# Start-up loads put in another order, and the bf16 copy of W1 made by casts inside DRAM

## The chip, the cores and the metric

The kernel runs on one core of a Trainium2 chip. The metric is the device time of one execution in microseconds (us). The engines are TensorE (PE in the profile; PEld is its weight load), VectorE (DVE), ScalarE (ACT), GpSimd (POOL) and SyncE (SP). GpSimd and SyncE issue the transfers here.

## The reference, cut to what matters

Grouped-query attention over 8 batches (16 query heads, 4 key/value heads, 384 tokens, head size 64), then a residual MLP block on the 1024 features:

```python
attn = softmax(q @ k.T / 8) @ v              # per batch and head; x = heads side by side
a1 = alpha1 * x + beta1
u  = x + lam * (w_tok @ a1)                  # token mixing, 384 x 384
a2 = alpha2 * u + beta2
out = u + lam * (relu(a2 @ W1) @ W2)         # W1: 1024 x 4096, W2: 4096 x 1024
```

All inputs are float32. The kernel computes in bf16, so W1, W2, q, k and v have to be cast, and it casts them on their way in, in the transfer.

## The kernel before: the parts that matter

Two Python generators are woven together. `side(b)` is attention, token mixing and the transposes of a2 for batch b; `main(b)` is the MLP of batch b, in two phases, h (a2 @ W1, 16 chunks of W1 in a ring of four buffers) and ch (h @ W2). Batch 0's `side` runs alone; then `main(b)` is woven with `side(b+1)`. W2 stays in SBUF. W1 does not fit, so batch 0 loads it as float32 with a cast and writes a bf16 copy to DRAM, which the later batches read.

```python
def load_qkv(b):
    ...  # k, q (four groups), v: GpSimd transfers that cast
    nc.gpsimd.tensor_copy(out=vt[b % 2][:, :, :, :D], in_=vr)
...
def load_w1(b, c):
    t = sb.tile([P, NDT, CW * P], bf, tag="w1", name="w1", bufs=4)
    if b == 0:
        nc.gpsimd.dma_start(out=t, in_=w1src[:, :, c * CW * P:(c + 1) * CW * P])
        nc.sync.dma_start(out=w1_scr[c], in_=t)
    else:
        nc.sync.dma_start(out=t, in_=w1_scr[c])
    return t
...
with tc.manual_schedule(engines={mybir.EngineType.PE}):
    for _ in side(0):
        pass
    for b in range(B):
        m = main(b)
        if b + 1 < B:
            qkv[b + 1] = load_qkv(b + 1)
            s = side(b + 1)
        if b == 0:
            ...  # W2 in eight pieces, all of it, before any W1 chunk
```

`manual_schedule` fixes the order of TensorE's instructions only. On every other engine the order is chosen when the program is built, from the dependences: an instruction that depends on nothing may be put far ahead of its place in the text. The hardware then executes each engine's list in order: the traces below show engines standing 5.9 to 35.2 us in front of one instruction with the others behind it.

The softmax here doesn't subtract the row's maximum and nothing guards it: scores larger than these inputs give would overflow.

## Time and profile before

| | us |
|---|---|
| median of the runs | 914.5 |
| batch 0's h starts | 72.5 |
| from there to batch 1's h | 128.3 |
| each later batch, from h to h | 104.1 |
| last batch's h to the end | 88.3 |

These rows add up to the span: 72.5 + 128.3 + 6 x 104.1 + 88.3 = 913.7 (913.5 in the trace). "h starts" is the first matmul of the first product for a batch in TensorE's timeline. The 104.1 is TensorE's own work (busy 103.2 of the 104 us from 200 to 304), so the first two rows are where time can be won or lost.

The list of TensorE's waits in the kernel before (what waited, for what; us in all, times, longest) has this line on W1:

```profile
PE h L276 <- DMA w<-in_moe_w_ch_dram: 21.4, 7, 5.5
```

It is by far the largest of TensorE's waits that is not in the first 13 us.

### The profile page before, as it was taken

The numbers are of one execution on the slowest core, as the hardware profiler recorded it, in microseconds if no ns is written. First come the engines' busy times: TensorE is split into PE (matmuls) and PEld (weight loads), VectorE is DVE, ScalarE is ACT, GpSimd is POOL, SyncE is SP. The second block draws the span as 40 slices with busy tenths as digits, with TensorE's granted clock in tenths as the row PEclk, the third lists the DMA queues.
The fourth block names the chain that finished last, engine by engine and source line by source line (L and its number), as shares of the span: only waits on it lengthen the run. The fifth ranks groups of instructions, "written<-read, shape, count | busy, mean of one in ns | idle before, by whom it ended". The sixth has DMA issues, their size and how long they took to land.

```text
span 913.5 us, 13365 instructions
## 1 busy us (share of the span) xinstructions
PE 846.7 (93%) x5753; PEld 470.2 (51%) x5753; DVE 415.6 (45%) x767; ACT 212.3 (23%) x321; POOL 68.1 (7%) x89
## 2 busy tenths in 40 slices
PE   2647778999999999999999999999999999999997
PEld 1414444456654565456654566445654566445543
DVE  2572332564346444464436543464436534372211
ACT  1602232004420243103420143103430044101100
POOL 6402220000000000001000000001000000000000
PEclk9957899999999999999999999999999999999999
DMA  9999997117511554107521455006620244104300
GB/s 197 196 211 204 232 247 205 44 42 189 171 58 44 119 171 147 44 24 184 171 81 44 97 170 170 24 36 157 177 102 24 71 159 155 44 35 154 135 34 37
DMA packets 72475, 109.69 MB, mean 120 GB/s; under 512 B 28640, under 2 KB 45024, under 8 KB 72416
## 3 DMA queue, kind: packets, MB, share of 16 engines
q1 hardware_dynamic: 26064, 82.32, 25.8%
q0 software_dynamic: 46352, 26.51, 21.4%
q8 instruction: 45, 0.74, 0.3%
q14 instruction: 14, 0.11, 0.0%
HBM read 114.36 MB, written 20.97 MB: 148 GB/s over the span
## 4 chain that ended last, share of the span: by engine, by line
PE 82%; DMA 12%; DVE 4%; issue 1%; POOL 0%; ACT 0%; POOLq 0%; ACTq 0%
PE ch L288 36%; PE h L276 31%; DMA w<-in_moe_w_ch_dram 7%; PE sc L203 6%; PE av L160 3%; DMA v_raw<-in_v_dram 3%; PE tok L244 2%; DVE kz L151 2%; DMA w_scr<-w 1%; DMA k_raw<-in_k_dram 1%; PE tp L191 1%; PE tp L262 1%; DVE o L293 1%; DVE k L141 0%; PE tp L146 0%
## 5 line engine op out<-in xcount | busy, mean ns | idle before, releaser
L276 PE MATMUL h<-a2T,w 128*128 128x384 bf16 x2048 | 376.4, 330 | 21.4 <-DMA w<-in_moe_w_ch_dram 21.4
L288 PE MATMUL ch<-w,hT 128*128 128x512 bf16 x1536 | 352.2, 379 | 0.9
L276 PEld LDWEIGHTS <-w 128*128 128x128 bf16 x2048 | 195.8, 99 | 146.3 <-DMA w<-in_moe_w_ch_dram 23.7
L288 PEld LDWEIGHTS <-hT 128*128 128x128 bf16 x1536 | 147.4, 98 | 168.0 <-issue 2.9
L206 ACT ACTIVATE es<-sc 128x768 bf16<-128x768 f32 x192 | 153.9, 809 | 200.3 <-PE sc L203 200.3
L279 ACT ACTIVATE hT<-h 128x384 bf16<-128x384 f32 x128 | 62.7, 490 | 453.0 <-PE h L276 453.0
L281 DVE TENSOR_SCALAR hT<-h 128x384 bf16<-128x384 f32 x128 | 71.3, 557 | 205.0 <-PE h L276 204.2
L203 PE MATMUL sc<-qT,kz 128*128 128x384 bf16 x384 | 95.4, 332 | 4.0 <-DVE qT L195 2.9
L293 DVE TENSOR_TENSOR o<-ch,lam 128x512 f32<-128x512 f32 x48 | 33.1, 690 | 117.2 <-PE ch L288 116.6
L160 PEld LDWEIGHTS <-es 128*128 128x128 bf16 x1152 | 53.2, 99 | 21.7 <-ACT es L206 1.5
L160 PE MATMUL av<-v,es 128*128 128x65 bf16 x1152 | 57.4, 195 | 1.5 <-ACT es L206 0.8
L167 DVE RECIPROCAL rinv<-av 128x6 f32<-128x6 f32 x64 | 12.3, 192 | 90.5 <-PE av L160 90.1
L203 PEld LDWEIGHTS <-kz 128*128 128x128 bf16 x384 | 36.0, 99 | 30.3 <-issue 4.6
L244 PE MATMUL tok<-a,wtokT 128*128 128x512 bf16 x144 | 42.3, 410 | 6.9 <-DVE a L178 6.9
L246 DVE TENSOR_TENSOR x<-tok,x 128x512 f32<-128x512 f32 x48 | 33.0, 689 | 28.3 <-PE tok L244 28.3
L170 DVE TENSOR_TENSOR x<-av,rinv 128x192 f32<-128x192 f32 x128 | 39.7, 352 | 1.9
L294 DVE TENSOR_TENSOR o<-o,x 128x512 f32<-128x512 f32 x48 | 35.8, 747 | 0.9
L87 POOL DMA_DIRECT2D q_raw<-in_q_dram x32 | 23.8, 747 | 149.8 <-DVE q L185 149.7
L178 DVE TENSOR_TENSOR a<-a1f,h 128x768 bf16<-128x768 f32 x32 | 30.6, 958 | 1.5 <-issue 0.5
L177 DVE TENSOR_TENSOR a1f<-x,g 128x768 f32<-128x768 f32 x32 | 30.6, 958 | 1.1
L250 DVE TENSOR_TENSOR a2f<-x,al 128x1024 f32<-128x1024 f32 x24 | 29.4, 1224 | 0.7
L251 DVE TENSOR_TENSOR a<-a2f,be 128x1024 bf16<-128x1024 f32 x24 | 29.3, 1222 | 0.5
(33 smaller groups left out, 221.4 us busy)
## 6 DMA issues: line engine op xcount, KB each, us to landing
w<-w_scr SPq DMA_DIRECT2D x112, 512.0 KB, 3.2
out_dram<-o SPq DMA_DIRECT2D x48, 256.0 KB, 2.0
w<-in_moe_w_ch_dram POOLq DMA_DIRECT2D x8, 1024.0 KB, 19.7
w<-in_moe_w_ch_dram POOLq DMA_DIRECT2D x16, 512.0 KB, 12.1
w_scr<-w SPq DMA_DIRECT2D x16, 512.0 KB, 5.8
q_raw<-in_q_dram POOLq DMA_DIRECT2D x32, 192.0 KB, 4.9
k_raw<-in_k_dram POOLq DMA_DIRECT2D x8, 192.0 KB, 4.3
v_raw<-in_v_dram POOLq DMA_DIRECT2D x8, 192.0 KB, 5.2
```

The lines of the kernel that those rows point to most:

```text
L160: nc.tensor.matmul(out=av[:, hh, sq, :], lhsT=es[sk][:, hh, sq * P:(sq + 1) * P], rhs=vb[:, hk, sk, :], start=(sk == 0), stop=(sk == NST - 1))
L170: nc.vector.tensor_tensor(out=x[:, :, c0:c0 + D], in0=av[:, hh, :, :D], in1=rinv[:, hh].to_broadcast([P, NST, D]), op=MUL)
L203: nc.tensor.matmul(out=sc[:, hh, :S], lhsT=kz[:, hk, hh, sk * P:(sk + 1) * P], rhs=qT[:, p % 2, :], start=True, stop=True)
L206: nc.scalar.activation(out=e, in_=sc[:, :, :S], func=EXP, scale=scale_qk)
L244: nc.tensor.matmul(out=ps, lhsT=wtokT[:, st, tt * P:(tt + 1) * P], rhs=a1[:, st, cs], start=(st == 0), stop=(st == NST - 1))
L246: nc.vector.tensor_tensor(out=x[:, tt, cs], in0=ps, in1=x[:, tt, cs], op=ADD)
L276: nc.tensor.matmul(out=ps[:, :S], lhsT=w1[:, dt, j * P:(j + 1) * P], rhs=a2T[:, dt, :], start=(dt == 0), stop=(dt == NDT - 1))
L279: nc.scalar.activation(out=hT[:, nt, :], in_=ps[:, :S], func=RELU)
L281: nc.vector.tensor_scalar_max(out=hT[:, nt, :], in0=ps[:, :S], scalar1=0.0)
L288: nc.tensor.matmul(out=ps, lhsT=hT[:, nt, ms * P:(ms + 1) * P], rhs=w2[:, nt, cs], start=(nt == 0), stop=(nt == NNT - 1))
L293: nc.vector.tensor_tensor(out=o, in0=ps, in1=lam_t[:, cs], op=MUL)
L294: nc.vector.tensor_tensor(out=o, in0=o, in1=x[:, ms, cs], op=ADD)
```

## The change

The intent: batch 0's q, k and v come first and nothing beside them; half of W2 is loaded before most of W1, the other half between the W1 chunks; the bf16 copy of W1 no longer holds the ring's buffers, since sixteen DRAM-to-DRAM casts make it, written after everything else of the start. The diff, cut to its core:

```diff
-    w1_scr = tc.dram_tile([NCH, P, NDT, CW * P], bf, name="w1_scr")
+    w1_scr = [tc.dram_tile([P, NDT, CW * P], bf, name=f"w1_scr{c}") for c in range(NCH)]
...
-        nc.gpsimd.tensor_copy(out=vt[b % 2][:, :, :, :D], in_=vr)      # in load_qkv
+        nc.vector.tensor_copy(out=vb[:, :, :, :D], in_=vr)             # in side(b)
...
-        nc.sync.dma_start(out=t, in_=src)                              # lam, alpha, beta
+        nc.gpsimd.dma_start(out=t, in_=src)                            # behind q, k, v
...
             nc.gpsimd.dma_start(out=t, in_=w1src[:, :, c * CW * P:(c + 1) * CW * P])
-            nc.sync.dma_start(out=w1_scr[c], in_=t)
...
+    w1_tiles = {c: load_w1(0, c) for c in range(RING)}                 # RING = 4
+    def late_loads():
+        for i in range(4):
+            load_w2(0, i, 4)
+        yield
+        for c in range(RING, NCH):
+            w1_tiles[c] = load_w1(0, c)
+            if c % 2 == 1:
+                load_w2(1, (c - RING) // 2, 8)
+            yield
+        for i in range((NCH - RING) // 2, 8):
+            load_w2(1, i, 8)
+        for c in range(NCH):
+            nc.gpsimd.dma_start(out=w1_scr[c], in_=w1src[:, :, c * CW * P:(c + 1) * CW * P])
...
-    wtok_in = sb.tile([P, NST, S], bf, tag="a1", name="wtok_in", bufs=1)
+    wtok_in = sb.tile([P, NST, S], bf, tag="o", name="wtok_in", bufs=2)
```

Besides, q's transposes are made one group ahead, a1 and a2 in smaller pieces, w_tok's transposes in the middle of batch 0's attention, and `main(0)` calls `next(late)` after each chunk.

More of the change, by code (lines that the diff above doesn't have):

```diff
@@ L56 @@
     NCH = NNT // CW
+    RING = 4
     scale_qk = 1.0 / float(D) ** 0.5
@@ L62 @@
     psum = ST(tc.psum_pool(name="psum", bufs=2))
-    w1_scr = tc.dram_tile([NCH, P, NDT, CW * P], bf, name="w1_scr")
+    w1_scr = [tc.dram_tile([P, NDT, CW * P], bf, name=f"w1_scr{c}") for c in range(NCH)]
     ident = const.tile([P, P], bf, tag="ident", name="ident")
-    make_identity(nc, ident)
     vt = [const.tile([P, Hkv, NST, D1], bf, tag=f"v{i}", name=f"v{i}") for i in range(2)]
-    for t in vt:
-        nc.vector.memset(t[:, :, :, D:], 1.0)
     w2 = const.tile([P, NNT, DM], bf, tag="w2", name="w2")
@@ L75 @@
     kz = const.tile([P, Hkv, 2, S], bf, tag="kz", name="kz")
-    nc.vector.memset(kz[:D, :, 1, :], 0.0)
-    nc.vector.memset(kz[D:, :, 0, :], 0.0)
     wtokT = const.tile([P, NST, S], bf, tag="wtokT", name="wtokT")
+    qkv = {}
     def load_qkv(b):
@@ L88, in load_qkv, with bcast @@
             qr.append(t)
-        vr = sb.tile([P, Hkv, NST, D], bf, tag="v_raw", name="v_raw", bufs=1)
-        nc.gpsimd.dma_start(out=vr, in_=v[b].rearrange("h (p st) d -> p h st d", st=NST))
-        nc.gpsimd.tensor_copy(out=vt[b % 2][:, :, :, :D], in_=vr)
-        return qr, kr
-    def bcast(ap, name, pool, tag, bufs=1):
-        t = pool.tile([P, DM], f32, tag=tag, name=name, bufs=bufs)
+            if g == 0:
+                vr = sb.tile([P, Hkv, NST, D], bf, tag="v_raw", name="v_raw", bufs=1)
+                nc.gpsimd.dma_start(out=vr, in_=v[b].rearrange("h (p st) d -> p h st d", st=NST))
+        qkv[b] = qr, kr, vr
+    def bcast(ap, name):
+        t = const.tile([P, DM], f32, tag=name, name=name)
         src = bass.AP(tensor=ap.tensor, offset=ap.offset, ap=[[0, P]] + [list(x) for x in ap.ap])
-        nc.sync.dma_start(out=t, in_=src)
+        nc.gpsimd.dma_start(out=t, in_=src)
         return t
-    qkv = {0: load_qkv(0)}
-    lam_t = bcast(moe_lam, "lam", const, "lam")
-    g1 = bcast(moe_alpha1, "g1", const, "g1")
-    h1 = bcast(moe_beta1, "h1", const, "h1")
-    nc.gpsimd.tensor_tensor(out=g1, in0=g1, in1=lam_t, op=MUL)
-    nc.gpsimd.tensor_tensor(out=h1, in0=h1, in1=lam_t, op=MUL)
-    al2 = bcast(moe_alpha2, "al2", const, "al2")
-    be2 = bcast(moe_beta2, "be2", const, "be2")
-    wtok_in = sb.tile([P, NST, S], bf, tag="a1", name="wtok_in", bufs=1)
-    nc.gpsimd.dma_start(out=wtok_in, in_=moe_w_tok.rearrange("(p tt) s -> p tt s", tt=NST))
     w1src = moe_w_ch1.rearrange("(dt di) nf -> di dt nf", di=P)
@@ L116, in load_w1 @@
     def load_w1(b, c):
-        t = sb.tile([P, NDT, CW * P], bf, tag="w1", name="w1", bufs=4)
+        t = sb.tile([P, NDT, CW * P], bf, tag="w1", name="w1", bufs=RING)
         if b == 0:
             nc.gpsimd.dma_start(out=t, in_=w1src[:, :, c * CW * P:(c + 1) * CW * P])
-            nc.sync.dma_start(out=w1_scr[c], in_=t)
         else:
@@ L123, in load_w1, with load_w2 @@
         return t
+    def load_w2(dw, i, n):
+        r, cs = slice(i * NNT // n, (i + 1) * NNT // n), slice(dw * 512, (dw + 1) * 512)
+        nc.gpsimd.dma_start(out=w2[:, r, cs], in_=w2src[:, r, cs])
+    load_qkv(0)
+    make_identity(nc, ident)
+    for t in vt:
+        nc.vector.memset(t[:, :, :, D:], 1.0)
+    nc.vector.memset(kz[:D, :, 1, :], 0.0)
+    nc.vector.memset(kz[D:, :, 0, :], 0.0)
+    g1 = bcast(moe_alpha1, "g1")
+    h1 = bcast(moe_beta1, "h1")
+    lam_t = bcast(moe_lam, "lam")
+    nc.vector.tensor_tensor(out=g1, in0=g1, in1=lam_t, op=MUL)
+    nc.vector.tensor_tensor(out=h1, in0=h1, in1=lam_t, op=MUL)
+    wtok_in = sb.tile([P, NST, S], bf, tag="o", name="wtok_in", bufs=2)
+    nc.gpsimd.dma_start(out=wtok_in, in_=moe_w_tok.rearrange("(p tt) s -> p tt s", tt=NST))
+    w1_tiles = {c: load_w1(0, c) for c in range(RING)}
+    al2 = bcast(moe_alpha2, "al2")
+    be2 = bcast(moe_beta2, "be2")
+    def late_loads():
[11 more added lines that the diff above has]
+            nc.gpsimd.dma_start(out=w1_scr[c], in_=w1src[:, :, c * CW * P:(c + 1) * CW * P])
     xs = {}
@@ L132, in side @@
     def side(b):
-        qr, kr = qkv.pop(b)
+        qr, kr, vr = qkv.pop(b)
         vb = vt[b % 2]
@@ L137, in side, with k_transpose @@
         a1 = sb.tile([P, NST, DM], bf, tag="a1", name="a1", bufs=1)
-        for h0 in range(0, Hkv, 2):
+        def k_transpose(h0):
             k2 = sb.tile([P, 2, NST, 2, D], bf, tag="q2", name="k2", bufs=1)
@@ L151, in side, with q_transpose @@
                 nc.vector.tensor_copy(out=kz[r, h0:h0 + 2, i, :], in_=pv[r])
-            yield
-        qT = None
-        av_todo = None
+        def q_transpose(g):
+            q2 = sb.tile([P, 2, NST, 2, D], bf, tag="q2", name="q2", bufs=1)
+            for i in range(2):
+                nc.vector.tensor_copy(
+                    out=q2[:, i],
+                    in_=qr[g][:, 2 * i:2 * i + 2].rearrange("p h st d -> p st h d"))
+            ps = tp_ps([P, 2 * NST, P])
+            for i in range(2 * NST):
+                hp, st = i // NST, i % NST
+                nc.tensor.matmul(out=ps[:, i, :], lhsT=q2[:, hp, st].rearrange("p h d -> p (h d)"),
+                                 rhs=ident, is_transpose=True, start=(i == 0),
+                                 stop=(i == 2 * NST - 1), skip_group_check=True)
+            qT = sb.tile([P, 2, S], bf, tag="qT", name="qT", bufs=2)
+            nc.vector.tensor_copy(out=qT.rearrange("p a b -> p (a b)"),
+                                  in_=ps.rearrange("p a b -> p (a b)"))
+            return qT
         def av_piece(p, es, hh, av):
@@ L171, in norm @@
                                         in1=rinv[:, hh].to_broadcast([P, NST, D]), op=MUL)
-            if p % 2 == 1:
-                sl = slice((p - 1) * P, (p + 1) * P)
-                t = sb.tile([P, NST, 2 * P], f32, tag="tmp", name="a1f", bufs=1)
-                gb = g1[:, None, sl].to_broadcast([P, NST, 2 * P])
-                hb = h1[:, None, sl].to_broadcast([P, NST, 2 * P])
-                nc.vector.tensor_tensor(out=t, in0=x[:, :, sl], in1=gb, op=MUL)
-                nc.vector.tensor_tensor(out=a1[:, :, sl], in0=t, in1=hb, op=ADD)
-        for p in range(NP):
-            if p % 2 == 0:
-                g = p // 2
-                q2 = sb.tile([P, 2, NST, 2, D], bf, tag="q2", name="q2", bufs=1)
-                for i in range(2):
-                    nc.vector.tensor_copy(
-                        out=q2[:, i],
-                        in_=qr[g][:, 2 * i:2 * i + 2].rearrange("p h st d -> p st h d"))
-                ps = tp_ps([P, 2 * NST, P])
-                for i in range(2 * NST):
-                    hp, st = i // NST, i % NST
-                    nc.tensor.matmul(out=ps[:, i, :], rhs=ident,
-                                     lhsT=q2[:, hp, st].rearrange("p h d -> p (h d)"), is_transpose=True, start=(i == 0),
-                                     stop=(i == 2 * NST - 1), skip_group_check=True)
-                qT = sb.tile([P, 2, S], bf, tag="qT", name="qT", bufs=2)
-                nc.vector.tensor_copy(out=qT.rearrange("p a b -> p (a b)"),
-                                      in_=ps.rearrange("p a b -> p (a b)"))
-                yield
+            sl = slice(p * P, (p + 1) * P)
+            t = sb.tile([P, NST, P], f32, tag="a1f", name="a1f", bufs=1)
+            gb = g1[:, None, sl].to_broadcast([P, NST, P])
+            hb = h1[:, None, sl].to_broadcast([P, NST, P])
+            nc.vector.tensor_tensor(out=t, in0=x[:, :, sl], in1=gb, op=MUL)
+            nc.vector.tensor_tensor(out=a1[:, :, sl], in0=t, in1=hb, op=ADD)
+        k_transpose(0)
+        yield
+        qTs = {0: q_transpose(0)}
+        yield
+        nc.vector.tensor_copy(out=vb[:, :, :, :D], in_=vr)
+        av_todo = None
+        for p in range(NP):
             hk = (2 * p) // G
@@ L203, in side @@
                     nc.tensor.matmul(out=sc[:, hh, :S], lhsT=kz[:, hk, hh, sk * P:(sk + 1) * P],
-                                     rhs=qT[:, p % 2, :], start=True, stop=True)
-                e = sb.tile([P, 2, S], bf, tag="es", name="es", bufs=6)
+                                     rhs=qTs[p // 2][:, p % 2, :], start=True, stop=True)
+                e = sb.tile([P, 2, S], bf, tag="es", name="es", bufs=5)
                 nc.scalar.activation(out=e, in_=sc[:, :, :S], func=EXP, scale=scale_qk)
@@ L217, in side @@
                     yield
+                if sk == 1 and p % 2 == 0 and p + 2 < NP:
+                    qTs[p // 2 + 1] = q_transpose(p // 2 + 1)
+                    yield
+                if sk == 0 and p == 1:
+                    k_transpose(2)
+                    yield
+                if sk == 1 and p == 3 and b == 0:
+                    for st in range(NST):
+                        ps = tp_ps([P, NST, P])
+                        wv = wtok_in.rearrange("p tt (s st) -> p tt st s", st=NST)
+                        for tt in range(NST):
+                            nc.tensor.matmul(out=ps[:, tt, :], lhsT=wv[:, tt, st, :], rhs=ident,
+                                             is_transpose=True, start=(tt == 0),
+                                             stop=(tt == NST - 1), skip_group_check=True)
+                        nc.vector.tensor_copy(out=wtokT[:, st, :],
+                                              in_=ps.rearrange("p a b -> p (a b)"))
             av_todo = (p, es, None)
@@ L224, in side @@
         norm(pp, av)
-        if b == 0:
-            for st in range(NST):
-                ps = tp_ps([P, NST, P])
-                wv = wtok_in.rearrange("p tt (s st) -> p tt st s", st=NST)
-                for tt in range(NST):
-                    nc.tensor.matmul(out=ps[:, tt, :], lhsT=wv[:, tt, st, :], rhs=ident,
-                                     is_transpose=True, start=(tt == 0), stop=(tt == NST - 1),
-                                     skip_group_check=True)
-                nc.vector.tensor_copy(out=wtokT[:, st, :], in_=ps.rearrange("p a b -> p (a b)"))
         yield "tok"
@@ L239, in side @@
         for tt in range(NST):
+            a2 = sb.tile([P, NDT, P], bf, tag="a2", name="a2", bufs=2)
+            a2s.append(a2)
             for dw in range(NDW):
@@ L246, in side @@
                 nc.vector.tensor_tensor(out=x[:, tt, cs], in0=ps, in1=x[:, tt, cs], op=ADD)
-                yield
-            a2f = sb.tile([P, DM], f32, tag="tmp", name="a2f", bufs=1)
-            a2 = sb.tile([P, NDT, P], bf, tag="a2", name="a2", bufs=2)
-            nc.vector.tensor_tensor(out=a2f, in0=x[:, tt, :], in1=al2, op=MUL)
-            nc.vector.tensor_tensor(out=a2.rearrange("p a b -> p (a b)"), in0=a2f, in1=be2, op=ADD)
-            a2s.append(a2)
+                a2f = sb.tile([P, 512], f32, tag="a2f", name="a2f", bufs=2)
+                nc.vector.tensor_tensor(out=a2f, in0=x[:, tt, cs], in1=al2[:, cs], op=MUL)
+                eng = nc.vector
+                eng.tensor_tensor(out=a2[:, dw * 4:(dw + 1) * 4, :].rearrange("p a b -> p (a b)"),
+                                  in0=a2f, in1=be2[:, cs], op=ADD)
+                yield
             if tt > 0:
@@ L269, in main @@
         x = xs.pop(b)
+        more = late if b == 0 else None
         for c in range(NCH):
-            w1 = load_w1(b, c)
+            w1 = w1_tiles.pop(c) if b == 0 else load_w1(b, c)
             for j in range(CW):
@@ L282, in main @@
                 yield
+            if more is not None:
+                next(more, None)
         for dw in range(NDW):
@@ L296, in main, with count @@
                 yield
+    def count(gen):
+        return sum(1 for _ in gen)
+    late = late_loads()
+    n_att = 2 + NP * NST + NP * 2 + NP // 2 - 1 + 1
+    n_main = NNT + 4 * NST * NDW
     with tc.manual_schedule(engines={mybir.EngineType.PE}):
@@ L301 @@
         for b in range(B):
-            m = main(b)
             s = None
             if b + 1 < B:
-                qkv[b + 1] = load_qkv(b + 1)
-                s = side(b + 1)
-            if b == 0:
-                for i in range(NNT // 4):
-                    nc.gpsimd.dma_start(out=w2[:, i * 4:(i + 1) * 4, :],
-                                        in_=w2src[:, i * 4:(i + 1) * 4, :])
-            n_main = NNT + 4 * NST * NDW
-            n_side = 2 + NP // 2 + NP * NST + NP * 2
-            done = 0
-            hold = False
+                load_qkv(b + 1)
+            if b == 0:
+                next(late)
+            m = main(b)
+            if b + 1 < B:
+                s = side(b + 1)
+            done, tok = 0, False
             for i, _ in enumerate(m):
@@ L317 @@
                     continue
-                want = min(n_side, (i + 1) * n_side * 14 // (n_main * 10))
-                while not hold and done < want + (1 if hold else 0):
-                    r = next(s, "end")
+                want = (i + 1) * n_att * 14 // (n_main * 10)
+                while not tok and done < want:
                     done += 1
-                    if r == "tok":
-                        hold = True
-                if done >= n_side and i >= n_main * 3 // 4:
-                    hold = False
+                    tok = next(s) == "tok"
+                if tok and i >= n_main * 3 // 4:
                     if next(s, "end") == "end":
```

## The prediction

> **What bounds the kernel now.** I read the page's busy slices first, then the chain of waits, then the timelines of the first 160 us. The slices:
>
> ```profile
> PE   2647778999999999999999999999999999999997
> PEclk9957899999999999999999999999999999999999
> DMA  9999997117511554107521455006620244104300
> ```
>
> A slice is 22.8 us. From slice 7 on TensorE is 90% busy or more: that part is TensorE's own work. The first six slices (137 us) are not, and there DMA stands at 9. So there are two kernels: a start bound by loading, and a long TensorE-bound run. In the chain of waits the groups of main's first product (line 276) start at 200.93, 305.01, 409.09, ... 825.40 us: one batch is exactly 104.08 us (54.1 for h, 50.0 for ch), with 99.2 us of each 100 busy. Nothing in the change touches that rate, so the question is when batch 1 starts its h, and the end follows 713 us later.
>
> The start, from the chain of waits:
>
> ```profile
> 1.27 11.31 DMA k_raw<-in_k_dram
> ...
> 33.12 21.79 DMA w<-in_moe_w_ch_dram
> 55.45 29.93 DMA v_raw<-in_v_dram
> ...
> 91.73 13.58 DMA w<-in_moe_w_ch_dram
> 105.33 5.87 DMA w_scr<-w
> 111.76 11.40 DMA w<-in_moe_w_ch_dram
> ```
>
> The reader is to see three things: the first k takes 11.31 us (the median k takes 4.3); weights are the wait from 33 us on; and from 91 us load, scratch copy and load alternate: a W1 buffer is free again only when its copy to scratch has been written. TensorE's timeline:
>
> ```profile
> 47.16 1.44 PE L244 MATMUL tok<-a,wtokT 128*128 128x512 bf16 x3 [3.23 <-DVE a L178]
> 52.23 4.00 PE L244 MATMUL tok<-a,wtokT 128*128 128x512 bf16 x9 [3.63 <-DVE a L178]
> ...
> 72.48 2.74 PE L276 MATMUL h<-a2T,w 128*128 128x384 bf16 x8 [5.51 <-DMA w<-in_moe_w_ch_dram]
> ```
>
> The token product waits for a1 on VectorE, because wtok_in holds the one "a1" buffer until it is transposed; then h waits for its first W1 chunk, queued behind all of W2. And GpSimd's timeline:
>
> ```profile
> 55.45 0.75 POOL L90 DMA_DIRECT2D v_raw<-in_v_dram  x1 [4.37 <-DMA w<-in_moe_w_ch_dram]
> 85.50 0.83 POOL L91 COPY v<-v_raw 128x768 bf16<-128x768 bf16 x1 [29.30 <-DMA v_raw<-in_v_dram]
> ```
>
> GpSimd stood 29.3 us in front of a copy whose v lay behind the weights in the queue; meanwhile it issued no W1 load.
>
> So batch 0's h starts at 72.48 and batch 1's at 200.93: 128.45 us where a steady batch takes 104.08, **24.4 us too much**. Those 24.4 and what can be cut from the 72.5 are all there is to win.
>
> **What the Trainium skill says.** "DMA: Bandwidth & Descriptors", section "Issuing engines are not separate DMA queues": transfers from any engine share the same 16 DMA engines. The trace agrees: the first k took 11.31 us while five broadcasts from SyncE (0.52 MB each) ran beside it. The same page, "SWDGE vs HWDGE vs iDMA": a cast can be issued only from GpSimd, so W1, W2, q, k, v and the new DRAM casts all stand in one queue and their order is what matters. The same page's Specifications give 435 GB/s as the fabric ceiling. From 50 to 60 us, with casts alone, the windows show 211 to 213 GB/s; that is counted in bf16 as landed (queue 0 shows 26.51 MB, which is W1, W2, q, k, v and w_tok at 2 bytes), so 422 GB/s of float32 read: at that ceiling. "TensorE: Matmul & The Clock Gate", Part 1: after idle windows of about 3.4 us the clock is halved. The trace agrees: granted 0.50 from 45 to 60 us, and three token products took 1.44 us.
>
> **The change, part by part.**
>
> *1. First exp.* It starts at 20.17. k (issued 1.27, median 4.3) should land near 5.6 once the broadcasts queue behind it; the identity now follows six issues of 0.75 us, so it is ready near 6.3. From k's landing to the first exp it was 20.17 - 12.58 = 7.6; the second k transpose moves later, and one such block is 15.44 - 13.02 = 2.4, which leaves 5.2. First exp about 12 (estimate): 8 us won.
>
> *2. Attention of batch 0.* ScalarE ran its 24 exps in 21.3 us (20.17 to 41.45). VectorE's share now has a1 in line: normalising 8 x (0.20 + 0.62) = 6.6; a1 in 16 halves of about 0.5 = 8; three q blocks of 0.60 + 0.55 = 3.5; k 0.61 + 1.12 = 1.7; wtokT 3 x 0.36 = 1.1; the v copy about 0.5. Sum 21.4, as much as the exps. I take 23: end at 35.
>
> *3. Token stage.* From 52.23 to the last copy's end at 67.70 it was 15.5 us, of which VectorE worked 13.5 (6 x 0.69, 6 x 1.22, 3 x 0.69). Halving the a2 pieces shortens only the dependence: 14.5, plus 1.5 for the last a1. h starts at 35 + 1.5 + 14.5 = **51 instead of 72.5: 21.5 us won**. W1's first four chunks (2.1 MB) come after 1.2 of q/k/v, 0.3 of w_tok and three broadcasts, so by about 26 us; they don't hold h.
>
> *4. Main of batch 0.* What must have landed before the last W1 chunk: q/k/v of two batches 2.4, w_tok 0.3, W1 8.4, half of W2 4.2 and six eighths of the other half 3.1, together 18.4 MB at 0.211 = 87 us; five broadcasts, 2.6 MB uncast at twice that rate, 6 us; from 1.3 that is 94.6. TensorE reaches chunk 15 at 51 + 15 x 3.38 = 101.7 (3.38 is 54.1 / 16). So the queue leads by some 7 us at the end; with a ring of four a load has three chunks, 10.1 us, to land, and one takes about 2 x 2.5 + 2. I allow 3 us of stalls: **24.4 - 3 = 21.4 us won**.
>
> *5. Casts to scratch.* They take the place of 16 copies from SBUF (8.4 MB, median 5.8 us each, in the ring's loop). 16 x 0.524 MB / 0.211 = 40 us after W2 is in, near 105: done near 145. Batch 1's main starts at 51 + 107 = 158. Hidden, with 13 us to spare.
>
> *6. The rest.* v's copy moves to VectorE (8 x about 0.5), a1 comes in smaller pieces, es has 5 buffers for 6: VectorE is 48% busy in a steady batch, so no effect; 104.1 stays.
>
> Sum: 914.5 - 21.5 - 21.4 = 871.6, so **872 us**.
>
> **Rivals.**
>
> *The casts go too early.* GpSimd's order is not the program's: v_raw of batch 2 was issued at 55.45, ahead of most of batch 0's W1, since nothing held it. The DRAM casts depend on nothing either. Were all ahead of the late W1 chunks, 40 us of transfers would be added: chunk 15 near 135, a stall of about 33 us, the whole near 902. Against it: the order before looks paced by transfer time (between two q_raw issues only one W2 piece), and the last W1 loads stand ahead in the program. I give it one chance in seven, and some in part.
>
> *The casts are slow or in the way.* No trace shows a DRAM-to-DRAM cast. At twice the time they end near 185; the W1 chunks themselves would still come in time, but batch 2's q and k stand behind them and TensorE, whose order is fixed, would wait up to 30 us at 158: about 895 to 900.
>
> *VectorE bounds the new start.* If its small pieces or their order cost more, h starts at 58 to 60: 880. For it: my 21.4 leaves no slack.
>
> *All is hidden anyway.* Against it: TensorE's idle time lies exactly in these 137 us, and the steady run can't absorb it.
>
> **Range and chances.** An h start between 46 and 57 gives 867 to 878; stalls of 0 to 15 us widen it to 862 to 890; the first two rivals pull the upper end to 896. Faster by over 2% needs under 896.2: 0.83. Within 2%: 0.14. Slower: 0.03, as nothing is added to the TensorE-bound run.
>
> **What would show it.** First exp near 12 us; first h near 51, not waiting for weights; in batch 0's main under 5 us of h waiting for W1; batch 1's h near 158 and each later one 104 us on; DRAM casts only after the last W1 load, done by 145, and no wait on k or q of batch 2. Wrong if casts stand among the W1 loads in GpSimd's timeline, or if VectorE has no idle time up to 35 us and h starts after 58.

## The result, and the profile after

The changed kernel takes **928.1 us** (median of four runs), against 914.3 for the kernel before in the same rounds. The ratio is 1.0152, with a 95% interval of 1.0135 to 1.0170. Ratios here are the mean time of one kernel's fast runs over the mean of the other's fast runs of the same rounds, so not quite the ratio of the medians quoted. The prediction was 872, with 896 as the upper end.

| us | before | predicted | after |
|---|---|---|---|
| batch 0's h starts | 72.5 | 51 | 61.8 |
| from there to batch 1's h | 128.3 | 107.1 | 151.7 |
| each later batch | 104.1 | 104.1 | 104.1 |
| last h to the end | 88.3 | - | 87.8 |

The start won 10.7 us; batch 0's main lost 23.4; the rest is as it was. First the busy slices of the page (TensorE, its granted clock, the transfers), which answer to the three lines shown of before:

```profile
PE   4675765999999999999999999999999999999997
PEclk9867898999999999999999999999999999999999
DMA  9999999205631175205631175105630144104301
```

The loading start is still there, still with a 9 for the transfers in every slice, and TensorE at 4 to 7 of ten in it. The windows of the changed kernel from 80 to 140 us (columns: window, busy time of PE, PEld, DVE, ACT and POOL, granted clock, DMA share, GB/s as landed) show what the transfers did in it:

```profile
80.00:100.00 20.00, 9.48 (x47) 4.89 (x47) 2.95 (x7) 3.42 (x5) 6.17 (x7) 0.66 1.45 198
100.00:120.00 20.00, 13.70 (x99) 8.16 (x100) 4.68 (x11) 4.18 (x7) 6.93 (x8) 0.91 1.45 198
120.00:140.00 20.00, 13.19 (x97) 7.64 (x95) 5.91 (x14) 4.59 (x8) 6.24 (x8) 0.91 1.45 198
```

The rate does not move, 198 GB/s in each window, so I take the queue to be full: 0.524 MB, one piece, every 2.65 us. What was in the queue is told by GpSimd's timeline (start, length, line, operation, in brackets the idle time before it and what ended it). Line 111 is W2, line 143 is a cast to the scratch copy, line 104 a W1 chunk, line 80 the k of batch 2:

```profile
57.97 0.74 POOL L111 DMA_DIRECT2D w<-in_moe_w_ch_dram  x1 [4.33 <-DMA w<-in_moe_w_ch_dram]
60.54 0.85 POOL L143 DMA_DIRECT2D w_scr<-in_moe_w_ch_dram  x1 [1.83 <-DMA w<-in_moe_w_ch_dram]
63.06 0.84 POOL L143 DMA_DIRECT2D w_scr<-in_moe_w_ch_dram  x1 [1.67 <-DMA w<-in_moe_w_ch_dram]
65.59 0.83 POOL L143 DMA_DIRECT2D w_scr<-in_moe_w_ch_dram  x1 [1.69 <-DMA w<-in_moe_w_ch_dram]
68.39 0.91 POOL L104 DMA_DIRECT2D w<-in_moe_w_ch_dram  x1 [1.97 <-PE tp L183]
70.69 0.84 POOL L143 DMA_DIRECT2D w_scr<-in_moe_w_ch_dram  x1 [1.40 <-DMA w<-in_moe_w_ch_dram]
...
126.36 0.84 POOL L143 DMA_DIRECT2D w_scr<-in_moe_w_ch_dram  x1 [1.79 <-DMA w<-in_moe_w_ch_dram]
...
131.90 0.76 POOL L80 DMA_DIRECT2D k_raw<-in_k_dram  x1
...
137.22 0.89 POOL L104 DMA_DIRECT2D w<-in_moe_w_ch_dram  x1 [2.14 <-DMA w<-in_moe_w_ch_dram]
```

The casts, last in the text of the start, are issued from 60.54 to 126.36 us; the last W1 chunk follows at 137.22. All sixteen casts, and all of W2, stand ahead of it. TensorE's timeline at the first chunks that were not there yet:

```profile
61.76 2.72 PE L308 MATMUL h<-a2T,w 128*128 128x384 bf16 x8 [0.78 <-DVE a2T L295]
88.92 2.74 PE L308 MATMUL h<-a2T,w 128*128 128x384 bf16 x8 [10.90 <-DMA w<-in_moe_w_ch_dram]
102.23 2.74 PE L308 MATMUL h<-a2T,w 128*128 128x384 bf16 x8 [3.84 <-DMA w<-in_moe_w_ch_dram]
```

Chunk 4 was issued at 68.39, as soon as its buffer was free, and h waited for it until 88.92: twenty us behind eight pieces of the queue. The first eight matmuls after such a wait take 2.74 us instead of 1.46, at half the clock (granted 0.50 from 89 to 92 us). And the changed kernel's list of TensorE's waits, against the 21.4 us shown of before:

```profile
PE h L308 <- DMA w<-in_moe_w_ch_dram: 27.5, 9, 10.9
PE h L308 <- DVE hT L313: 9.4, 1, 9.4
```

The second line is another thing. h does not wait for VectorE to be done with work but for VectorE to be free, and VectorE's timeline says what held it (line 218 is v's copy, line 162 k's):

```profile
34.36 0.36 DVE L218 COPY v<-v_raw 128x768 bf16<-128x768 bf16 x1 [5.91 <-DMA v_raw<-in_v_dram]
...
152.38 0.61 DVE L162 COPY k<-k_raw 128x384 bf16<-128x384 bf16 x2 [13.24 <-DMA k_raw<-in_k_dram]
```

At 34.36 this is the copy of batch 1's v, in the middle of batch 0's attention; at 152.38 the copy of batch 2's k, in batch 0's main. Both had been put early on VectorE, and VectorE stood in front of them until the transfers landed. The Trainium skill says in "TensorE: Matmul & The Clock Gate", in its table of specifications, that the queues of ScalarE, VectorE and GpSimd are strictly first in, first out; these 5.91 and 13.24 us of standing still agree.

### The profile page after: what moved, and what is told of

Read it like the earlier page. It is cut to its first block, busy times and chain, and to the rows that moved or that the text cites. A ratio compares the mean times of both kernels' runs of the same rounds, so it can differ in the third digit from the quotient of the medians.

```text
span 925.8 us, 13415 instructions
## 1 busy us (share of the span) xinstructions
PE 848.0 (92%) x5706; PEld 473.1 (51%) x5753; DVE 429.2 (46%) x889; ACT 212.0 (23%) x321; POOL 76.9 (8%) x104
## 4 chain that ended last, share of the span: by engine, by line
PE 80%; DMA 14%; DVE 3%; issue 1%; POOL 1%; POOLq 0%
PE ch L322 34%; PE h L308 32%; DMA w<-in_moe_w_ch_dram 7%; PE sc L226 5%; PE av L195 3%; DMA k_raw<-in_k_dram 2%; DMA w_scr<-in_moe_w_ch_dram 2%; PE tok L275 2%; DMA be<-in_moe_beta_dram 2%; DVE o L327 1%; PE tp L183 1%; PE tp L293 1%; DMA h<-in_moe_beta_dram 1%; DVE kz L172 1%; DVE a2f L279 1%
## 5 line engine op out<-in xcount | busy, mean ns | idle before, releaser
L308 PE MATMUL h<-a2T,w 128*128 128x384 bf16 x2048 | 378.4, 331 | 37.6 <-DMA w<-in_moe_w_ch_dram 27.5
L322 PE MATMUL ch<-w,hT 128*128 128x512 bf16 x1490 | 347.4, 379 | 6.6 <-DVE o L327 3.2
L195 PEld LDWEIGHTS <-es 128*128 128x128 bf16 x1152 | 53.9, 100 | 29.3 <-DVE x L205 7.7
L211 DVE TENSOR_TENSOR a1f<-x,g 128x384 f32<-128x384 f32 x64 | 35.6, 557 | 1.8
L212 DVE TENSOR_TENSOR a<-a1f,h 128x384 bf16<-128x384 f32 x64 | 35.6, 556 | 1.8
L281 DVE TENSOR_TENSOR a<-a2f,be 128x512 bf16<-128x512 f32 x48 | 33.0, 690 | 1.4
L279 DVE TENSOR_TENSOR a2f<-x,al 128x512 f32<-128x512 f32 x48 | 32.9, 688 | 1.0
L328 DVE TENSOR_TENSOR o<-o,x 128x512 f32<-128x512 f32 x48 | 33.0, 687 | 0.7
## 6 DMA issues: line engine op xcount, KB each, us to landing
w<-in_moe_w_ch_dram POOLq DMA_DIRECT2D x24, 512.0 KB, 20.4
```

What stands on the lines that cost most here:

```text
L195: nc.tensor.matmul(out=av[:, hh, sq, :], lhsT=es[sk][:, hh, sq * P:(sq + 1) * P], rhs=vb[:, hk, sk, :], start=(sk == 0), stop=(sk == NST - 1))
L211: nc.vector.tensor_tensor(out=t, in0=x[:, :, sl], in1=gb, op=MUL)
L279: nc.vector.tensor_tensor(out=a2f, in0=x[:, tt, cs], in1=al2[:, cs], op=MUL)
L308: nc.tensor.matmul(out=ps[:, :S], lhsT=w1[:, dt, j * P:(j + 1) * P], rhs=a2T[:, dt, :], start=(dt == 0), stop=(dt == NDT - 1))
L322: nc.tensor.matmul(out=ps, lhsT=hT[:, nt, ms * P:(ms + 1) * P], rhs=w2[:, nt, cs], start=(nt == 0), stop=(nt == NNT - 1))
```

## The experiments

Two theories followed from this. A: sixteen casts of 2.65 us each in front of the late W1 chunks are the loss. A': besides, VectorE is held by copies whose data stand behind the weights. The rivals: the ring of four is too short for loads that take 20 us to land (B), or W2's second half, which also went ahead of chunk 4, is to blame (C). All twelve runs gave correct results. They ran in four groups on different chips (1 to 4, 5 to 8, 9 to 11, and 12); the kernel before, timed beside each group, took 913.0 to 914.2 us, so medians of different groups compare to about 1 us.

| kernel | median us | ratio to before | h of batch 0 | to batch 1's h | later batches |
|---|---|---|---|---|---|
| before | 913.0 to 914.5 | 1 | 72.5 | 128.3 | 104.1 |
| after | 928.1 | 1.0152 | 61.8 | 151.7 | 104.1 |
| 1 casts held back | 897.8 | 0.9827 | 62.1 | 121.4 | 104.1 |
| 2 GpSimd in written order | 944.8 | 1.0347 | 61.4 | 145.1 | 104.1 to 113.3 |
| 3 no scratch copy | 899.4 | 0.9844 | 62.1 | 121.4 | 104.1 |
| 4 scratch copy from SBUF | 913.1 | 0.9992 | 67.0 | 133.0 | 104.1 |
| 5 k and v copies held | 939.0 | 1.0286 | 56.4 | 155.6 | 106.0 |
| 6 casts, and copies held | 899.4 | 0.9851 | 56.1 | 118.5 | 106.0 |
| 7 written order, copies held | 897.9 | 0.9835 | 56.5 | 111.6 | 111.6, then 106.0 |
| 8 before, with casts | 936.9 | 1.0258 | 73.5 | 151.1 | 104.1 |
| 9 all three held | 889.8 | 0.9730 | 55.8 | 116.9 | 106.0, then 104.1 |
| 10 and constants early | 885.7 | 0.9696 | 54.4 | 116.7 | 106.0, then 104.1 |
| 11 half the casts | 915.8 | 1.0021 | 60.8 | 136.6 | 104.1 to 105.8 |
| 12 four W2 pieces ahead | 889.7 | 0.9732 | 51.6 | 121.4 | 106.0, then 104.1 |

**1. The casts held back.** `tc.issue_after` adds an order on the issuing engine and no wait for completion:

```diff
+            with tc.issue_after(last_w1[0]):      # batch 0's last W1 load
                 nc.gpsimd.dma_start(out=w1_scr[c], ...)
```

> The changed kernel with one edge added: the sixteen DRAM-to-DRAM casts may be issued only after batch 0's last W1 load. Theory A (the casts stand among the late W1 loads and each 0.5 MB of them delays the next chunk by about 2.6 us, 40 us in all): h's wait for W1 falls from 27.5 us to under 10, batch 1's h starts near 170 instead of 213.6, total 880 to 890. Rival B (a ring of four with loads that land 20 us after issue is the limit whatever stands in the queue): h still waits over 20 us and the total stays above 905. Rival C (W2's second half, still ahead of chunk 4, is what delays): one wait of some 7 us at chunk 4 stays, the rest goes.

897.8 us: 30.3 us less than the changed kernel, and all of it between batch 0's h and batch 1's (151.7 to 121.4). No wait of h for W1 is left in TensorE's list, so B falls: the ring of four is enough when the queue holds only what is needed (run 7 shows it without the long wait that follows here). C's 7 us did not show either, since something else came first. One wait is left, here in TensorE's timeline and then VectorE's:

```profile
80.81 0.82 PE L186 MATMUL tp<-ident,q 128*128 128x128 bf16 x6 [14.36 <-DVE q L180]
```

```profile
78.98 0.37 DVE L221 COPY v<-v_raw 128x768 bf16<-128x768 bf16 x1 [16.94 <-DMA v_raw<-in_v_dram]
```

VectorE stood 16.94 us in front of batch 2's v, whose transfer had been issued at 60.71 behind W2. That is why the total stayed above the 880 to 890 that I expected.

**2. GpSimd in the order of the text.**

```diff
-    with tc.manual_schedule(engines={mybir.EngineType.PE}):
+    with tc.manual_schedule(engines={mybir.EngineType.PE, mybir.EngineType.Pool}):
```

> The changed kernel with GpSimd's instructions kept in the order in which the program is written: W2's second half goes between the W1 chunks and the casts come last. Theory A: as with the casts held back, 875 to 888; if W2's second half ahead of chunk 4 matters too (rival C), some 7 us less than the run with the casts held back alone. Rival B: above 905. A risk: q of batch 1 holds GpSimd up before W2 is issued.

944.8 us, the slowest of all, where I had expected 875 to 888, though W1's waits are down to 3.6 us in all, with the casts last and W2's second half between the chunks. From its list of waits:

```profile
PE tok L275 <- DVE x L277: 32.7, 1, 32.7
PE h L308 <- DVE hT L313: 19.8, 5, 6.8
PE h L308 <- DMA w<-in_moe_w_ch_dram: 3.6, 3, 1.5
```

Batch 2's k, q and v now came after sixteen casts (k issued at 156.24), but VectorE's list, still ordered by the build, had the copies of that k and v ahead of batch 1's token stage:

```profile
175.29 0.35 DVE L162 COPY k<-k_raw 128x384 bf16<-128x384 bf16 x1 [35.15 <-DMA k_raw<-in_k_dram]
```

VectorE stood still for 35.15 us. The order of one engine had been fixed and the other engine's had not followed. The six later batches together lost 27 us more (651.8 against 624.6 in run 1), with h waiting for VectorE five times (second line). Run 7 tests this reading.

**3. No scratch copy at all.** Every batch loads W1 from float32 with a cast:

```diff
-        if b == 0:
+        if True:
             nc.gpsimd.dma_start(out=t, in_=w1src[...])
-        for c in range(NCH):
-            nc.gpsimd.dma_start(out=w1_scr[c], ...)
```

> The changed kernel without any scratch copy: every batch loads W1 from float32 with a cast on GpSimd's queue (40 us of transfers in a batch of 104). Theory A: batch 0 as with the casts held back, total 880 to 890 if the later batches keep 104.1 us. If the casting loads of the later batches come late (GpSimd waits in front of a ring slot and holds k and q back), 895 or more with waits in every batch. Rival B: above 905.

62.1, 121.4 and 104.1, the same to 0.1 us as with the casts held back. So casts that come late cost nothing (the 880 to 890 that I expected are missed here as in run 1), and next to nothing is gained by them either: in a batch of 104 us the casting loads of W1 are as well hidden as the bf16 loads. Only the stretch after the last h is longer, 89.9 us against 87.8.

**4. The scratch copy from SBUF, as before.** All of the change except the casts:

```diff
             nc.gpsimd.dma_start(out=t, in_=w1src[...])
+            nc.sync.dma_start(out=w1_scr[c], in_=t)
-        for c in range(NCH):
-            nc.gpsimd.dma_start(out=w1_scr[c], ...)
```

> The changed kernel with the scratch copy as it was before (each chunk is written out from SBUF by SyncE, which holds its ring slot until written); all else changed. Theory A: the 40 us of casts are gone from the queue, 4.2 MB of writes in SBUF's direction remain in the way: four chunks per some 19 us as before, so h ends near 62 + 75 and the total is 890 to 905, between the held casts and the kernel before. Rival B predicts the same or worse than the changed kernel, 925 or more.

913.1: the same as the kernel before (interval 0.9972 to 1.0012), and not the 890 to 905 that I expected. Two waits on VectorE account for most of it, 9.4 us in batch 0's attention and 13.0 in its main, where VectorE stood 10.86 and 17.15 us in front of copies of v that stand early; W1's waits are 9.7 us in eleven pieces. Of the change, then, the casts cost 15 us (928.1 to 913.1) and all the rest together won about nothing.

**5. The copies of k and v held at their written place, the casts left early.**

```diff
+        pin = tc.keep_in_program_order if b > 0 else (lambda i: i)
-                nc.vector.tensor_copy(out=k2[:, i], ...)
+                pin(nc.vector.tensor_copy(out=k2[:, i], ...))
-        nc.vector.tensor_copy(out=vb[:, :, :, :D], in_=vr)
+        pin(nc.vector.tensor_copy(out=vb[:, :, :, :D], in_=vr))
```

> The changed kernel, with only VectorE's copies of the next batch's k and v held at their written place (they had been put early on VectorE, which then stood still until those transfers landed); the casts stay among the W1 loads. Theory A' (two causes that add: early casts, and VectorE held by copies whose data stand behind the weights): the 4.5 us wait in batch 0's attention and the 9.4 us wait of h on VectorE go, the 27.5 us wait for W1 stays: 910 to 918. Rival (the casts alone are the cause, VectorE's waits are only where the same delay shows): no change, 925 to 929.

A miss in both directions: 939.0. h starts 5.3 us earlier (the 5.91 us in the attention are gone) and yet batch 1's h starts at 212.1, 1.4 us earlier than in the changed kernel. Its list of waits:

```profile
PE h L309 <- DMA w<-in_moe_w_ch_dram: 36.5, 9, 14.8
```

The wait for W1 grew from 27.5 to 36.5 us: what TensorE won by starting early and by VectorE's being free, it spent waiting for the queue. While the casts are early, transfers set the end of batch 0's main, and a free VectorE brings little. The changed kernel's trace says the same: its last W1 chunk landed at 156.0 us and the product on that chunk began at 159.6, so freeing VectorE could win 3.6 us there at most. And each later batch takes 106.0 instead of 104.1, 1.9 us in every one: there the early place was the better one, since k has long landed when its copy is due; TensorE's timeline shows 0.91 us of it as a wait of k's transpose for that copy, once in each of these batches.

**6. Both holds.** Runs 1 and 5 together.

> Both: casts only after the last W1 load, and the copies of k and v at their written place. Theory A': against the 897.8 of the casts held back alone, the 14.4 us wait on a q copy behind v's copy and the 3.8 us in batch 0's attention go: 876 to 884. Rival (once VectorE is free, h waits for chunk 4 behind W2's second half instead): 888 to 898 with 7 us or more of waits for W1.

899.4, where I expected 876 to 884. Batch 1's h starts at 174.6, 9.0 us before run 1's 183.5, so A' holds for the start; but the hold costs 6 x 1.92 = 11.5 us in the later batches. And the rival was right too: with VectorE free, chunk 4 is late behind W2's second half.

```profile
PE h L312 <- DMA w<-in_moe_w_ch_dram: 8.5, 2, 8.1
```

That 8.1 us is C's effect, hidden in run 1 by the longer wait on VectorE.

**7. GpSimd in written order, and the copies held.**

> GpSimd in written order, and the copies of k and v on VectorE at their written place. If the 32.7 us wait of the token stage in the run with GpSimd's written order came from such a copy alone: 905 to 915 or less. If batch 2's q and k, issued after sixteen casts, land too late in any case (near 175): a wait of 5 to 12 us at the start of batch 1's main is left, total 882 to 895.

897.9 against run 2's 944.8: the 32.7 us wait is gone, which confirms the reading of run 2. Batch 0 to batch 1 takes 111.6, the shortest of all runs, with 3.0 us of waits for W1. What is left at batch 1's start is the wait that I had named as a rival in the prediction:

```profile
173.97 0.82 PE L168 MATMUL tp<-ident,k 128*128 128x128 bf16 x6 [4.46 <-DVE k L163]
```

Batch 2's k, issued behind sixteen casts, is 4.5 us late; with this and the hold's 1.9 us a batch the total stays just above the 882 to 895 expected.

**8. The casts alone, on the kernel before.**

```diff
-            nc.sync.dma_start(out=w1_scr[c], in_=t)
...
+        if b == 0:                                # after main's last W1 chunk
+            for c in range(NCH):
+                nc.gpsimd.dma_start(out=w1_scr[c], in_=w1src[...])
```

> The kernel before with only its scratch copies replaced by sixteen DRAM-to-DRAM casts, written after batch 0's last W1 chunk; load order, v copy and all else as before. Theory A: nine of the casts are issued before chunk 4 and the rest among the loads, so the part alone costs time: 920 to 945. Rival (taking the copy out of the ring's loop helps more than the early casts cost): under 914.

936.9 us. Batch 0's main goes from 128.3 to 151.1 us; all else stays within 1 us. The casts cost 22.8 us here, without any other part of the change, and TensorE's wait for W1 grows from 21.4 us by about as much:

```profile
PE h L275 <- DMA w<-in_moe_w_ch_dram: 44.8, 10, 18.5
```

**11. Half the casts** (before 9 and 10, since it closes the question). In the changed kernel, only the even chunks go through the scratch copy; the odd ones are loaded with a cast in every batch:

```diff
-        if b == 0:
+        if b == 0 or c % 2 == 1:
...
-        for c in range(NCH):
+        for c in range(0, NCH, 2):
             nc.gpsimd.dma_start(out=w1_scr[c], ...)
```

> The changed kernel with half the casts: only the even W1 chunks go through the scratch copy, the odd ones are loaded from float32 with a cast in every batch (which kept 104.1 us a batch in the run without scratch). Nothing is held back. Theory A (bytes of early casts): batch 0 to batch 1 takes 121.4 us with no casts early and 151.7 with sixteen; with eight, about halfway, 132 to 141, total 906 to 916. Rival (it is one particular wait, such as batch 2's k behind the casts, and not their bytes): near one of the two ends, under 902 or over 921.

136.6 us from batch 0's h to batch 1's. With none of the casts early it was 121.4, with sixteen 151.7; the middle of the two is 136.55. Each early cast costs (151.7 - 121.4) / 16 = 1.9 us, of the 2.65 it takes in the queue. So the loss goes with their number, and not with one particular wait.

**9. All three held, with the copies held for batches 1 and 2 only.**

```diff
+        pin = tc.keep_in_program_order if b in (1, 2) else (lambda i: i)
             if c % 2 == 1:
-                load_w2(1, (c - RING) // 2, 8)
+                with tc.issue_after(last_w1[0]):
+                    load_w2(1, (c - RING) // 2, 8)
```

> The changed kernel with all three holds and no cost in later batches: casts after the last W1 load, W2's second half behind the W1 chunks it was written after, and the copies of k and v at their written place for batches 1 and 2 only (for all batches it cost 1.9 us in each). Theory A': h of batch 0 near 56, batch 1's near 164 to 168, batch 2's 106 later, then 104.1 each: 876 to 886, and no wait for W1 of more than 3 us. Rival (W2's second half ahead of chunk 4 does not matter): the 8 us wait at chunk 4 shows up elsewhere, total 887 or more.

889.8: 2.7% under the kernel before, though over the 876 to 886 expected. The miss is in batch 0's main, 116.9 us. GpSimd stood in front of chunk 4's buffer with all else behind it (first line), and the queue ran empty meanwhile (DMA share and GB/s in the two windows of the second fence):

```profile
62.54 0.96 POOL L106 DMA_DIRECT2D w<-in_moe_w_ch_dram  x1 [28.52 <-PE tp L189]
```

```profile
55.00:60.00 5.00, 4.23 (x18) 2.38 (x18) 2.03 (x5) 0.49 (x1) 0.00 (x0) 0.50 0.23 37
60.00:65.00 5.00, 5.00 (x32) 2.93 (x31) 2.71 (x8) 1.20 (x2) 2.46 (x4) 0.84 0.14 10
```

The Trainium skill says in "DMA: Bandwidth & Descriptors", section "Anatomy of one DMA — SWDGE (gpsimd) path", that DMA engines do not wait on semaphores, that a wait is made by the issuing sequencer before dispatch. This trace agrees: one load's wait for a buffer kept every later load out of the queue for 28.5 us. In the changed kernel W2's second half filled this stretch (line 111, issued from 34.62 to 57.97 us), and the casts came after it.

**10. The start mended besides.** The identity is made before the first loads, and lam, alpha1 and beta1 are issued before the last two q groups (a few lines moved).

> As the run before, and the start mended: the identity is made before the first loads are issued, and the broadcasts of lam, alpha1 and beta1 are issued before the last two q groups. If the 3.3 us wait of the second k transpose (VectorE waiting for lam ahead of the k copy) and the late identity are on the path: h of batch 0 at 52 to 55, total 2 to 4 us below the run before. If batch 0's start is set by the chain of exps and VectorE's 21 us of work instead: no change within 1 us.

**885.7 us, the fastest: 3.0% under the kernel before (interval 0.9668 to 0.9724), and by the medians 4.6% under the changed one.** The waits aimed at are gone: the first transpose starts at 5.54 us instead of 6.95, and the 3.1 us at the second k transpose are no more. h starts 1.4 us earlier, which is no more than single profiles of one start differ by (60.8 to 62.1 in the changed kernel and runs 1, 3 and 11). Of the 4 us between the medians the profiles show 2.4 (spans of 888.0 and 885.6); the profiled execution of run 10 was its slowest, 1.6 us above its median.

**12. Four pieces of W2's second half ahead of chunk 4**, to fill the empty queue of runs 9 and 10.

> As the run with the holds and the constants early, but four of the eight pieces of W2's second half may go ahead of W1 chunk 4, and four stay among the chunks. In the two runs before, GpSimd stood 28.5 us in front of chunk 4's ring slot with everything else behind it and the queue ran dry. If those idle transfers are why h still waits 5.7 us for W1: that wait falls under 2 us, batch 1's h comes 3 to 6 us earlier, total 879 to 883. Rival (the pieces ahead delay chunk 4 as much as they save later): within 2 us of 885.7.

889.7: a miss, 4 us slower. The queue is full now (206 to 208 GB/s from 55 to 65 us), but chunk 4, issued at 57.17 behind those pieces, is late:

```profile
71.59 2.74 PE L318 MATMUL h<-a2T,w 128*128 128x384 bf16 x8 [3.15 <-DMA w<-in_moe_w_ch_dram]
```

W1's waits rose from 5.7 to 9.6 us. h started 2.8 us earlier than in run 10, and the queue took that back. Nothing in the traces ties the earlier start to the edit: the first nine transfers are issued at the same times within 0.01 us in both profiles, but lam took 6.6 us to land here and 8.4 in run 10, and from 18 to 23 us TensorE's granted clock was 1.00 here and 0.66 there. What made these differ is not shown. Somewhere between zero and four pieces may be a better number; I did not search for it.

## Why the prediction was wrong

**What bounds the kernel: right.** The later batches take 104.1 us in the changed kernel as before, the end follows batch 1's h by some 712 us in both, and the first 160 us decide.

**Step 4 failed, and it is the main error.** It listed "what must have landed before the last W1 chunk" as 18.4 MB, in the order of the text. The trace has 28.2 MB there: the last quarter of W2's second half (1.05), sixteen casts (8.4) and batch 2's k and one q (0.4) more. At 0.2 MB per us these 9.8 MB are 49 us; less the lead of 7 us that the step had found, 42 us of delay, where batch 0's main missed its 107.1 us by 44.6. That the two come so close is partly luck: the last W1 chunk landed at 156.0 us, 12.4 later than 94.6 + 49 (in part because the queue moved 198 to 207 GB/s and not 211), and h had started 10.8 later than the step assumed, which made up for most of it. The way of adding was sound, but it was done on the wrong order. Its other part, that a ring of four is enough for loads that land in 7 us, held in run 1 and in run 7, with 3.0 us of waits for W1 where I had allowed 3.

**The rival that came true had been written down, and its chance misjudged.** I gave the early casts one in seven because the issue order of the kernel before "looks paced by transfer time", so that the late W1 loads would stand ahead. Half of that is true: the casts were not all issued at once, they alternate with the chunks. But pacing does not help when the chunk's buffer is taken and the cast needs none. In GpSimd's list a cast stands where GpSimd would otherwise have stood at a ring slot, and the next chunk comes behind it (read off the list; how the build decides was not looked into). The evidence was in the profile that I quoted: batch 2's v_raw at 55.45 us, ahead of chunk 4. The size given for it, "a stall of about 33 us", was close to the 30.3 us that run 1 gives back. Its total, near 902, was still 26 us short: h started 10.8 us later than assumed, and batch 0's main took 151.7 us where that stall would give 137.1.

**Step 5** took the casts as a stretch of 40 us after W2. Their duration is right: 2.65 us each, against 2.5 for the same piece loaded to SBUF (198 and 206 GB/s), so one half of the second rival (slow casts) is refuted. Its other half, k and q of batch 2 behind the casts, is seen: 13.2 us in front of VectorE's copy of k in the changed kernel, 4.5 us of TensorE in run 7. The place of the casts is wrong, by the same error.

**Steps 1 to 3: right in kind, 10.8 us too optimistic.** The first exp started at 12.63 (predicted 12). The token stage took 16.8 us, from 44.94 to 61.76 (predicted 16). The term that failed is the attention, 23 us predicted, 32 measured (12.6 to 44.9). TensorE lost 4.5 us where VectorE waited for batch 1's v; that hold taken away, h starts at 56.4 (run 5). Another 2.65 us went at the second k transpose, behind g1's product on VectorE, which waited for lam until 15.96 us. I had summed VectorE's work and not asked what it would stand in front of.

**Step 6** said that v's copy on VectorE has no effect. In the later batches that is right. In the start the 29.3 us in which GpSimd stood in front of v's copy were not removed by moving the copy but in part moved with it: VectorE stood 5.9 and 3.6 us in front of copies of v in the changed kernel and 16.9 in run 1. (The 13.2 us are in front of a copy of k, which was on VectorE before.)

**Slips that did not decide.** The busy line shows seven slices (160 us) under 9, not six (137). Five pieces of W2's second half, not six, stand ahead of the last chunk in the text: 0.5 MB or 2.5 us less. And 862 as the lower end does not follow: an h start of 46 with no stalls gives 864.

What stays open: by which rule the build places an instruction without dependences, and why the same first transfers land at different times in runs 10 and 12.

## What to carry to other kernels

Before adding up what lies in a queue, find out who decides its order: a transfer that depends on nothing has no place of its own and will be put wherever its engine would otherwise stand, ahead of the ones that you need, so give it a dependence or an explicit order. A wait that is moved to another engine is still a wait; look for what the new engine has behind it. And once a start is bound by the queue, nothing won on the engines shows until the queue holds only what is needed next.

## What the Trainium skill lacked or had wrong

- "DMA: Bandwidth & Descriptors" ties casts to GpSimd but gives no rate for them. The runs show 198 to 213 GB/s counted as bf16 landed, twice that as float32 read, and nearly the same for a cast from DRAM to DRAM as for one to SBUF: 198 GB/s with such casts in the queue, 206 with loads to SBUF alone.
- The same page, in "Where 436 GB/s comes from", says that for transfers between HBM and SBUF the HBM side, about 358 GB/s, binds. On this single core the casting loads read 2 x 211 = 422 GB/s (an estimate from the 211 GB/s landed), near the page's fabric figure instead. What the sentence lacks is a condition: the page's own measured rates, which it calls single-core numbers, pass 358 too.
- The same page fits one transfer as 2.0 us plus its bytes over the bandwidth. Nothing is said of how long a queue GpSimd builds up: pieces of 0.5 MB took 20.4 us (median) from issue to landing in the changed kernel, about eight of them deep at 2.65 us each.
- No page on DMA or on reading traces warns that a transfer without dependences may be issued long before its place in the program. Here casts written after the last W1 load (issued at 137.22 us) were issued from 60.54 us on, which cost 30.3 us.
